# Two interleaved transformer layers on one core: V's weights arranged in finer pieces, early partial sums of layer 2 in one step, and new order tables

## The chip, the cores and the metric

The kernel runs on one core of one Trainium2 chip. The metric is device time in microseconds of one execution; lower is better. The core has five engines that run side by side, each in the order in which its instructions were written: TensorE (PE, matrix products; its weight loads are listed apart as PEld), VectorE (DVE), ScalarE (ACT), GpSimd (POOL) and SyncE (SP), which here only issues DMA transfers. They wait for one another through semaphores. A DMA transfer runs beside the engines once SP has issued it.

## The reference

The reference applies two layers to x, 2048 tokens of 512 values, each layer an attention block and a token-mixing MLP, with the same weights in both layers:

```python
x = A_x
x = x + _A_ref(_layernorm(x), A_wqkv, A_wo)
x = x + _B_ref(_layernorm(x), B_w1, B_b1, B_w2, B_b2)
x = x + _A_ref(_layernorm(x), A_wqkv, A_wo)
x = x + _B_ref(_layernorm(x), B_w1, B_b1, B_w2, B_b2)
```

`_A_ref` forms Q, K and V with one product (512 by 1536), splits them into 32 heads of 16, and lets each token attend to itself and the 255 tokens before it: scores times 16^-0.5, mask, softmax, weighted sum of V, and the output product with `wo` (512 by 512). `_B_ref` normalises again (the MLP's input is thus normalised twice), multiplies along the tokens, `u = gelu(w1^T h + b1)` with 1792 rows, and back to 2048 tokens, `y = w2^T u + b2`. All arrays are bf16.

## The kernel before

**How an order is written.** The kernel first records every operation in an object `Plan`: which engines could do it, what it reads and writes, and a priority. Nothing is run in the order of recording. A table `ORDER` (L27 on) holds, for each of the five engines, the list of its operations in the order in which they are to run, each operation's number packed into two characters. `arrange` decodes it, and `emit` writes every engine's instructions in that order and puts a semaphore wait before an operation for what it needs from others. So the order of the work, and which of two or three possible engines does an operation, is fixed by this table; the priorities in the code have no effect once the table is there. A second table, `BANKS`, says which of two spare PSUM banks (6 or 7) each use of a spare bank gets, and `misc_bank` (L476) hands them out.

**Attention.** The tokens are handled in four quarters of 512 (Q = 0 to 3), the heads in four tiles of eight heads (t = 0 to 3), and each pair of quarter and tile in nine steps (m = 0 to 8) over blocks of keys. For a step, `emit_scores` (L651) lets PE multiply K and Q into one of two score buffers of two PSUM banks each; `emit_exp` (L670) lets ACT exponentiate 128x1024 of them into `p_sb` (L672), after which DVE or POOL multiplies the edges of the window with 0 or 1 (L689); `emit_pv` (L697) multiplies with V, to which columns of ones are joined so that the sums of the softmax come out of the same product. After a tile's nine steps, the two result banks are copied to `oU` and `o2` (called `oU` and `o` in the profile) by `copy_out` (L332 on DVE, L334 on ACT). Every second tile, three small DMA transfers collect the sums into `den_c` and one of 256 KB moves rows of `o` into `oU`; the next copy into `o` waits for it. `job_inverse` (L734) and `job_normalise` (L744) divide, `job_outproj` (L625) multiplies with `wo` and adds to x. In between, `job_k`, `job_q` and `job_v` (L523, L529, L573) make K, Q and V of the next tile or quarter with `project` (L498), from the normalised tokens that were turned by DMA (`job_transpose`, L482) or, for the first quarter, by PE. The masked copies of K and Q stand at L514 (DVE) and L519 (ACT); V is copied to `vT`, turned 32 by 32 (L578) and spread into its tile (`spread_v`, L557; L563 DVE and POOL, L568 ACT).

**Weights of V.** The columns of V's weights have to stand in another order of heads than in memory. They are loaded as they are into a part of `w1buf`, and `turn_weights` (L407) copies them into `wqkv`, one operation for each chunk of 128 input values (c = 0 to 3), each of two instructions (r = 0, 1). `project` for V reads all four chunks and so waits for all four operations.

**MLP.** The 1792 rows are 14 tiles of 128 (`ft`). A tile's sum runs over all 2048 tokens, so over the four quarters. `u_product` (L826) makes four matmuls for each quarter. For six tiles (`NPART = 6`), the parts of the first two quarters are summed early, while the attention still runs on the later ones (`job_u_part`, L842): step 0 multiplies quarter 0 and copies the bank into room in `uT`; step 1 multiplies quarter 1 and adds bank and copy into `part`, which the profile calls `v_all` (L851). `job_u` (L864) later adds the rest (L872) and applies gelu (L875). For eight other tiles three quarters are summed ahead in PSUM. `job_y` (L878) makes the 16 token tiles of the result (matmul L900, addition to x at L904). Of layer 1's 16 tiles, the later ones run inside layer 2's attention. w1 comes in halves of 512 KB (`w1_half_dma`, L807) and pieces of 256 KB (`w1_dma`, L802), w2 in pieces of 896 KB (`w2_dma`, L822), into buffers that K, Q, the turned tokens and `oU` have left.

Of the kernel before, what the change touches and what calls it, by code (L numbers as in the profile page):

```python
# [8 lines left out]
ACTF = mybir.ActivationFunctionType  # L9

P = 128
# [4 lines left out]
NPART = 6  # L16
# [13 lines left out]
AoApAqArAsBHBJAtAuAvBLBNBPAwC-BTDiBRBVBnDRCcBzCaCmBrChAxC1CwCsBvC7DCClB3CvDIDMC0C6DVDBDHDLDcDTEDDkDqEcEwGODvDZD2FCF0DgDpDuEAD7DzEID1END6GgEYD-EHEMEhER  # L30
FXEnEsHJE1EgE6EmE-ErE0FHE5FMG5FTE+FGFLFaHjFQFvF2HWF7FZGAFuFzGGGKF6F-GRGFGJGQGUGbGqGjGiGnIAGtGmG0GsGzG3G7IOHAG-HEJbHMHDHLHTHQHYHcHgHpHsHbHfHwHoH4JzH9Hv
IGIyILH3H8IaJnIeIFIKImITKkIqIvHzI4IdIhIpIuI9I3I8JCJTJAKSJgJYIiJsK9JkJXJdJ4KuJwJjJrKJJvJ3J7J8LNKVKIKNLZKnKMKUKfKYLnKxKrM-KmK4MDK-KqKwLENGLIK3K7LQMQLWLD
LfLHLvLPLTLkLsNJLzLeLjL7LrLyLbMAL6L-MINQMNNeMbMfNoMHMnMMMUMrNuMvMeMiM3MqMuL2M8NCOlMjNLNVM2OMM7NbNBNlNIMyNrNSNzNOPkNaN3OENkNiNqOINyN2ORNYOcODOHOOOgOVQW
OnOrPLOyOfOkOqO4OxO1O-O3PDPaPIOPPQO+PXPTPCPHPNPdPhO8PrPWPcPwP2PmPgPqP+PvP1QFQmQPP9QTQ9QZQEQIQdP5QiQSQYQtRVQzQcQhQ3QqRBQsRIQyQ2Q8RMQCRSRFRaRPRfRLRRRkRZ
ReRjRyRxR1SpR2R3SyS1SzSqS2S4S5SBS0SsSEStSvSPSLS3STSHSrSwSjSxSuSkS-TLTBTFTMTDS6SlTPTbTTTcTUTfTQTgS7TXTYSmSnSoS9TJTHTuT+TzT0TvT5T6UnUoT-UiUMUjUVUTUNURUX
UbUZUgUcU0VKVAYVWbYWWcVTVOU4U8VhVcXwXxVIVSVmVtVZVEVyVbVgV2V7VlV+VsWFWgWwVxV1WSWNVqXPV9WjWCWXW+WoWtWJWRWWZeW-W6WiWnW1ZUWLXLXUWsW0XiXZW5XEXeYpX5XnXTXYXd
XsXmXrX2ZtYDX+aDYKX1YRZCYkX9YCYHYraEYwYOY1YQY6YjYoYvY0Y5Y9Y+ZFa0ZXZPZEa1abZIZbZhbeZoZvZWbfZ0ZaZgZnZ4cBaAZrZzaLa9aUZ3Z-aIaYbLahaTaXaoagaQawanava5a6aOZ9
bDbIcEbXbbdPbobCbHbQbscFbwbabjb5akb+brbvb4cRdhcWb9cecDcVcbcicxbkcqcubzcZc2chcpc6cldHctc1dLdsc5dSdGdcd7dkdKdRdpdVeLardvd2djeXd9dodud1eCekeGd5eOfBeUeBeF
edf+eheNepeRexeZe5ecegeoe+hMfGewe4fLe9fFesfZfKfSfdfOflgtfpftgde0f1fcfgfof7gNgBfsf0gKfhgUf6gAgagHgRgkhlingqgygFg2gZgjgphDfwhHgxg1hRiLhchChGhOhghVhngIhP
hrhyh8hfh4hkhqh-gPiDhxh3iIh1iQiXh+iTiCidiHiNihjWiriWiwicigiqi2ivi1iki+i9jEjFghjPjIjTiai5jZjdjmjijSjYjcjhjtgXjsjzj3gnjykIkVkBj2j8kFkSj9kMkfjCjqkakLkykR  # L40
kZkekjkkkPlykxk1k2k3lplzlsl1l4l2lvlEl5lwlBl0ltlHlLl6lTlPlxl3ljlklulllqmBmLmMmDlrmFmbmXmfl-mYmgmTmPmQmUmclmlnlol9l7mHmJmrm0m1mwmnmomxm9msnCm5m6nGnDnHm+
nPnTnLnMnQnUnXnbnfnnncngnjnYnqnk""",
    "vector": """
AaAbAUAcAYAdAZAzAeA1A0A2A7ASA+A5A3A6AfAWBEA9A4BBBABbBIBGBDBXBMBdBZBaAXAVBcAOBeBYAPAnATBfBhDjBSBWBjDSBpCbBsBqBtC3BuFgBwCkBxFeByCzB5DFB6FkFhFfFiFlEFEGEe
FjFmDKEfDaEyDfDPFDFoF1EzFqD0ECD+GhETEaESJDFYEbFEEqJFE8JEHKJGG6JHFVFRFSJJHkF5JIHXGDHlGWJKGVGrGTJNJLGdGlHmGpIBICGvGwGxIPG9G2G+JcHHHRHaHZHSHtHuIEHeHiJ0Hr
H6H7IQIzIRHyIIINISJ1IVJoI0IUKlIxI6H0JpJBKTIjI7JqJ2H1JPJeJfKvK+H2IkIlJ6J+KALOLaKZKCLoLpKpKEKhKtMEK0NAMFK6NHK1MRLSLYLwLVLhLULxNKLdLcNRMGL+NfNpMVMWMhMpNv
NwMSL3M6MTOmMxNxMtMkL4ONL5MzNTNgNPMlN1NnNhMmNjN6N7N9PlNZOWOKOBOAOTN-OLOiOCQXPMOuOvOtO2O6OwO7PBPFPbOQPKPVPGPUPPPOO9PZPfPSPtPoPnP4M0QnQHQoPzQRM1QKQJQ+RW
# [21 lines left out]
lilgmmmjmkmum3mqnBnAnJm4nSm8nFnWnenOnKmvnpnamznsninm""",  # L69
}  # L70
BANKS = (
    "76767676767667767776667767676767676666777667676766776777766676667666667767776766677777766766776677776676767776767776766666676666776767677677"
    "667666777767667676776677776677676777776676667677666667676767767666")


# [957 lines left out]
```

## Time and profile before

| what | us |
|---|---|
| median of 3 runs | 493.44 (492.94 to 494.23) |
| profiled execution, its own time | 493.72 |
| its span, first to last instruction | 492.0 |
| busy: PE / DVE / ACT / POOL | 467.4 / 339.1 / 322.5 / 192.1 |
| layer 1's attention ends, its MLP begins | about 163 |
| layer 2's attention begins to fill / ends | about 229 / 399 |
| TensorE clock granted | 1.0 throughout |

The span is shorter than the execution by 1.7 us, which lie around it. A group's line of the profile gives the line of the kernel, the engine, the operation, what it writes and reads, the count, the busy time in us and the mean duration of one in ns, and then the idle time just before these instructions with what ended it. A line of waits gives who waited for whom, the sum in us, how many times, and the longest. A line of windows gives the stretch and, for PE, PEld, DVE, ACT and POOL, the busy time and the instructions, then the granted clock, the share of the DMA engines and GB/s. The chain that ended last goes back from the end to what released each step.

### The profile page before, as it was taken

What the parts mean: (1) busy time and instruction counts of PE and PEld (TensorE: products, weight loads), DVE (VectorE), ACT (ScalarE), POOL (GpSimd) and SP (SyncE); (2) the same over time, 40 slices, a digit from 0 to 9 for tenths busy, and PEclk for the clock granted to TensorE, in tenths of its full rate; (3) what the DMA queues carried; (4) which work ended last, traced back from release to release, by engine and by line L of the source; (5) the groups of instructions that cost most, each with busy time, mean ns of one, the idle gap of its engine ahead of it and who ended that gap; (6) DMA issues with size and microseconds to landing.
All of it is one profiled execution on the core that took longest, in us unless ns stands there. A gap on an engine that the chain in (4) does not pass through costs nothing.

```text
span 492.0 us, 17498 instructions
## 1 busy us (share of the span) xinstructions
PE 467.4 (95%) x7610; PEld 255.9 (52%) x7706; DVE 339.1 (69%) x716; ACT 322.5 (66%) x394; POOL 192.1 (39%) x364
## 2 busy tenths in 40 slices
PE   8989889999999999999999999999999999999997
PEld 7444555555555444444445455555556554444444
DVE  7999999988897460246789868899878756121213
ACT  6889999999999303502688798999999940440000
POOL 5979775853314210002645513576354230000000
PEclk9999999999999999999999999999999999999999
DMA  6513319203013671505022500030300677050672
GB/s 214 87 66 79 81 5 113 69 6 112 27 46 92 181 223 50 151 0 151 2 44 79 141 27 3 29 53 19 112 15 16 182 211 217 23 151 0 174 201 96
DMA packets 82412, 43.61 MB, mean 89 GB/s; under 512 B 18720, under 2 KB 81312, under 8 KB 82336
## 3 DMA queue, kind: packets, MB, share of 16 engines
q1 hardware_dynamic: 78464, 42.48, 31.9%
q0 software_dynamic: 3872, 0.02, 1.5%
q8 instruction: 60, 0.98, 0.8%
q14 instruction: 16, 0.13, 0.1%
HBM read 32.51 MB, written 2.10 MB: 70 GB/s over the span
## 4 chain that ended last, share of the span: by engine, by line
PE 69%; DVE 14%; issue 5%; DMA 4%; ACT 4%; POOL 2%; SPq 1%; DVEq 0%; ACTq 0%; POOLq 0%
PE ps L832 19%; PE ps L900 18%; PE ps L503 10%; PE ps L661 9%; PE ps L710 8%; PE ps L630 4%; ACT p_sb L672 3%; DVE stats L439 2%; DMA oU<-o 2%; PE ps L754 1%; DVE q_sb L514 1%; DVE vT L332 1%; POOL p_sb L689 1%; DMA w1buf<-in_B_w_dram 1%; DVE vB L578 1%
## 5 line engine op out<-in xcount | busy, mean ns | idle before, releaser
L672 ACT ACTIVATE p_sb<-ps 128x1024 bf16<-128x1024 f32 (+8 forms) x288 | 261.0, 973 | 25.7 <-PE ps L661 20.4
L689 POOL TENSOR_TENSOR p_sb<-p_sb,edge 128x128 bf16<-128x128 bf16 (+2 forms) x233 | 107.4, 476 | 135.7 <-ACT p_sb L672 114.4
L661 PE MATMUL ps<-q_sb,k_sb 64*64 64x288 bf16 (+8 forms) x2816 | 106.6, 250 | 2.5 <-ACT p_sb L672 2.0
L503 PE MATMUL ps<-xhT,wqkv 128*128 128x512 bf16 x330 | 84.6, 380 | 7.0 <-issue 4.6
L710 PE MATMUL ps<-p_sb,v_all 64*64 64x288 bf16 (+8 forms) x2816 | 88.4, 246 | 2.6 <-DVE o L332 1.4
L661 PEld LDWEIGHTS ps<-q_sb,k_sb 64*64 64x64 bf16 x2816 | 52.9, 106 | 55.0 <-ACT p_sb L672 34.4
L710 PEld LDWEIGHTS ps<-p_sb,v_all 64*64 64x64 bf16 x2816 | 59.5, 107 | 15.2 <-issue 5.7
L900 PE MATMUL ps<-uT,w1buf 128*128 128x512 bf16 x272 | 62.4, 379 | 0.8 <-issue 0.5
L904 DVE SCALAR_TENSOR_TENSOR x_sb<-ps,b2col,x_sb 128x512 bf16<-128x512 f32 x31 | 22.6, 746 | 55.8 <-PE ps L900 55.7
L503 PEld LDWEIGHTS ps<-xhT,wqkv 128*128 128x128 bf16 x376 | 30.8, 97 | 39.3 <-issue 6.1
L689 DVE TENSOR_TENSOR p_sb<-p_sb,edge 128x256 bf16<-128x256 bf16 (+2 forms) x167 | 39.8, 257 | 9.6 <-ACT p_sb L672 7.8
L832 PE MATMUL ps<-xh_sb,w1buf 128*128 128x512 bf16 x175 | 43.3, 380 | 2.4 <-issue 1.5
L439 DVE BATCH_NORM_STATS2 stats<-x_sb 128x6 f32<-128x512 bf16 x64 | 43.0, 680 | 0.8 <-DMA x_sb<-in_A_x_dram 0.3
L900 PEld LDWEIGHTS ps<-uT,w1buf 128*128 128x128 bf16 x280 | 26.5, 98 | 32.2 <-issue 1.1
L514 DVE TENSOR_TENSOR q_sb<-ps,even 128x1024 bf16<-128x1024 f32 (+1 forms) x31 | 36.4, 1180 | 3.0 <-PE ps L503 2.5
L469 ACT ACTIVATE xh_sb<-x_sb,shift,rstd 128x512 bf16<-128x512 bf16 x9 | 7.2, 808 | 46.0 <-POOL shift L463 32.8
L459 POOL TENSOR_TENSOR rstd<-vare,mhalf 128x4 f32<-128x4 f32 x15 | 15.4, 1027 | 55.1 <-DVE nmean L461 48.3
L514 DVE TENSOR_TENSOR k_sb<-ps,half 128x1024 bf16<-128x1024 f32 x27 | 32.7, 1212 | 3.0 <-PE ps L503 2.1
L900 PE MATMUL ps<-uT,oU 128*128 128x512 bf16 x149 | 34.4, 379 | 0.3
L630 PE MATMUL ps<-wo_sb,oT 128*128 128x512 bf16 x113 | 29.4, 380 | 2.2 <-issue 1.3
L832 PE MATMUL ps<-xh_sb,k_sb 128*128 128x512 bf16 x124 | 30.2, 379 | 0.6 <-ACT p_sb L672 0.4
L832 PEld LDWEIGHTS ps<-xh_sb,w1buf 128*128 128x128 bf16 x192 | 16.9, 98 | 21.7 <-issue 1.9
(88 smaller groups left out, 461.9 us busy)
## 6 DMA issues: line engine op xcount, KB each, us to landing
w1buf<-in_B_w_dram SPq DMA_DIRECT2D x10, 896.0 KB
oU<-in_B_w_dram SPq DMA_DIRECT2D x6, 896.0 KB
w1buf<-in_B_w_dram SPq DMA_DIRECT2D x10, 512.0 KB
oU<-o SPq DMA_DIRECT2D x16, 256.0 KB
k_sb<-in_B_w_dram SPq DMA_DIRECT2D x16, 256.0 KB
q_sb<-in_B_w_dram SPq DMA_DIRECT2D x8, 256.0 KB
xhT<-in_B_w_dram SPq DMA_DIRECT2D x8, 256.0 KB
out_dram<-x_sb SPq DMA_DIRECT2D x15, 128.0 KB
```

The source lines that it names most:

```text
L439: dve(lambda e: e.bn_stats(stats[:, t, :], x_sb[:, t, :]), 690, prio, reads=[R("x", t)], writes=[R("stats", t)])
L459: pool(lambda e: e.tensor_tensor(rstd[:, sl], vare[:, sl], mhalf[:], op=ALU.pow), 1000, prio, reads=[R("vare", g), R("mhalf")], writes=[R( ...
L503: last = e.matmul(ps[:, b, :], lhsT=wqkv[:, c, c0:c0 + P], rhs=xhT[:, buf, c, :], start=(c == 0), stop=(c == 3))
L514: return e.tensor_tensor(dst, src.unsqueeze(2).to_broadcast([P, n, 2, w]), mask[:].unsqueeze(1).unsqueeze(3).to_broadcast([P, n, 2, w]), o ...
L630: last = e.matmul(ps[:, b, :], lhsT=oT[:, buf, t, i * P:(i + 1) * P], rhs=wo_sb[:, t, :], start=(t == 0), stop=(t == 3))
L661: last = e.matmul(ps[64 * c:64 * c + 64, 2 * half + r, 32 * i0:32 * i1], lhsT=k_sb[rows, ring, t, kb % 16, :], rhs=q_sb[rows, t, c, 32 * i ...
L672: latest[0] = plan.op({ACT: (170 + int(2 * (512 - c0) * 0.84), lambda e: e.activation(p_sb[:, slot, :, c0:512], ps[:, 2 * half:2 * half + ...
L689: return e.tensor_tensor(v, v, g, op=ALU.mult)
L710: last = e.matmul(ps[64 * r:64 * r + 64, B_O + (c ^ r), 32 * i0:32 * i1], lhsT=v_all[rows, col:col + 64], rhs=p_sb[rows, slot, r, 32 * i0: ...
L832: r = e.matmul(ps[:, b, :], lhsT=blk[:, n, (ft % 2) * P:(ft % 2 + 1) * P], rhs=xh_sb[:, 4 * g + n, :], start=(first and g == quarters[0] a ...
L900: r = e.matmul(ps[:, b, :], lhsT=blk[:, fc, (st % 2) * P:(st % 2 + 1) * P], rhs=uT[:, fc, :], start=(fc == 0), stop=(fc == NFT - 1))
L904: dve(lambda e: e.scalar_tensor_tensor(x_sb[:, st, :], ps[:, b, :], b2col[:, st:st + 1], x_sb[:, st, :], op0=ALU.add, op1=ALU.add), 750, prio,
```

## The change

Three things change.

- `turn_weights` is called for each head tile t and half r, eight operations of one instruction instead of four of two; a V projection reads the two of its own tile.
- In layer 2, the six early tiles have one step instead of two: the matmuls of quarters 0 and 1 go into the same bank, one after the other, and one copy takes the sum to `part`. In layer 1 the two steps stay. `NPART` becomes `NPARTS = (6, 6)`, one number for each layer.
- `ORDER` and `BANKS` are new throughout, for all five engines: other positions, and other engines for some operations. Only the first lines of SP's list are shown. Its first loads were, in order, x tiles 0, 1, 2 to 3, 4 to 7, then the weights of K, of V and of Q; they are now x tiles 1, 2 to 3, 0, then Q's weights, x tiles 4 to 7, K's and V's weights.

```diff
-NPART = 6
+NPARTS = (6, 6)
...
     "sync": """
-AAABACAGADAFAECqCgCuCrDhDQDoC5DGHIG4GeEUGfEXEVEWElGZGYGXGaDUK8KjIWIXHPLMIZIYKiKbKcKdKeKRMXMZMYItMaLiOYOZOaObPuP0QLQlQOQgQMPpQNRdQxRiR6R7R8R9OUGEOjRwTs
+ABACAAAEAGADAFCkCyDUCuDlCvC9DKG8GjEYGiEbHMDsEaEZDYGcGbGdGeKmEpIaIcKnIdIbGIHTLQLAKVKhKgKfKiMbMdMcMeOYOdOcOeOfIxPyQPQRQkQSQQPtP4QpRhR+Q-R-SASBRmSkOnR0Sl
...
-        def turn_weights(c):
-            d = wqkv[:, c, 2 * D:3 * D].rearrange("p (t a r d) -> p t r a d", t=4, a=4, r=2)
-            o = w_nat[:, c].rearrange("p (t r a d) -> p t r a d", t=4, r=2, a=4)
-
-            def f(copy):
-                def g(e):
-                    for r in range(2):
-                        last = copy(e)(d[:, :, r], o[:, :, r])
-                    return last
-                return g
-            plan.op({DVE: (500, f(lambda e: e.tensor_copy)), POOL: (1000, f(lambda e: e.tensor_copy)),
-                     ACT: (900, f(lambda e: lambda a, b: e.activation(a, b, ACTF.Copy)))},
-                    reads=[R("w1", 2, 0)], writes=[R("wqkv", 2, c)], prio=-96)
-        for c in range(4):
-            turn_weights(c)
+        def turn_weights(t, r):
+            d = wqkv[:, :, 2 * D + t * P:2 * D + (t + 1) * P].rearrange("p c (a r d) -> p c r a d", a=4, r=2)[:, :, r]
+            o = w_nat[:, :, t * P + 64 * r:t * P + 64 * r + 64].rearrange("p c (a d) -> p c a d", a=4)
+            plan.op({DVE: (250, lambda e: e.tensor_copy(d, o)), POOL: (400, lambda e: e.tensor_copy(d, o)),
+                     ACT: (360, lambda e: e.activation(d, o, ACTF.Copy))},
+                    reads=[R("w1", 2, 0)], writes=[R("wqkv", 2, t, r)], prio=-96)
+        for t in range(4):
+            for r in range(2):
+                turn_weights(t, r)
...
-            pe(f, 866, prio, reads=([R("wqkv", 2, c) for c in range(4)] if which == 2 else [R("wqkv", which)]) + [R("xhT", buf, i) for i in range(4)],
+            pe(f, 866, prio, reads=([R("wqkv", 2, (c0 - 2 * D) // P, r) for r in range(2)] if which == 2 else [R("wqkv", which)]) + [R("xhT", buf, i) for i in range(4)],
...
-        def job_u_part(ft, step, prio):
+        def job_u_part(ft, step, prio, whole=False):
...
-            u_product(ft, b, (PARTQ[step],), prio, late=[R("xh", sc) for sc in range(4 * PARTQ[step], 4 * PARTQ[step] + 4)])
-            if step == 0:
+            quarters = PARTQ if whole else (PARTQ[step],)
+            u_product(ft, b, quarters, prio, late=[R("xh", sc) for q in quarters for sc in range(4 * q, 4 * q + 4)])
+            if whole:
+                copy_out(part, ps[:, b, :], b, prio, 680, [R("part", ft)] + held)
+            elif step == 0:
                 copy_out(early, ps[:, b, :], b, prio, 680, kept)
...
-            for ft in range(NPART):
-                todo.append((base + 55 + 0.5 * ft, lambda p, ft=ft: job_u_part(ft, 0, p)))
-                todo.append((base + 60 + UP0 + UPD * ft, lambda p, ft=ft: job_u_part(ft, 1, p)))
+            for ft in range(NPARTS[L]):
+                if L == 0:
+                    todo.append((base + 55 + 0.5 * ft, lambda p, ft=ft: job_u_part(ft, 0, p)))
+                todo.append((base + 60 + UP0 + (20 / NPARTS[L] - 0.03) * ft, lambda p, ft=ft, L=L: job_u_part(ft, 1, p, L == 1)))
```

By the decoded tables the instructions of PE (7708) and SP (178) stay as many; DVE has 727 for 718, ACT 395 for 396, POOL 351 for 368. The lines of the changed kernel behind L425 are smaller by about five.

## The prediction

> **What bounds the kernel now.** First the page's busy line, then the windows by stage, then the waits, the groups with shapes kept apart, and the chain of work that ended last. [...] Of the page's first part:
>
> ```profile
> PE 467.4 (95%) x7610; PEld 255.9 (52%) x7706; DVE 339.1 (69%) x716; ACT 322.5 (66%) x394; POOL 192.1 (39%) x364
> ```
>
> The windows (PE, PEld, DVE, ACT, POOL busy in each stretch) show the stages:
>
> ```profile
> 10.00:20.00 10.00, 9.65 (x100) 5.44 (x99) 9.85 (x25) 8.55 (x16) 9.25 (x22) 1.00 0.18 44
> 20.00:40.00 20.00, 17.81 (x298) 9.02 (x295) 19.59 (x41) 17.87 (x28) 17.32 (x39) 1.00 0.43 87
> 40.00:60.00 20.00, 17.56 (x415) 10.13 (x418) 18.72 (x42) 18.08 (x23) 17.18 (x38) 1.00 0.31 81
> 60.00:80.00 20.00, 18.35 (x516) 11.45 (x512) 18.15 (x38) 19.57 (x23) 12.52 (x19) 1.00 0.31 44
> ...
> 163.00:205.00 42.00, 41.68 (x252) 18.99 (x253) 15.68 (x30) 12.15 (x19) 3.85 (x6) 1.00 0.57 161
> ...
> 320.00:350.00 30.00, 28.41 (x748) 17.36 (x758) 28.05 (x55) 29.02 (x33) 19.66 (x35) 1.00 0.21 41
> 350.00:380.00 30.00, 28.48 (x768) 17.38 (x766) 24.64 (x51) 28.31 (x32) 16.26 (x30) 1.00 0.17 47
> 380.00:399.00 19.00, 18.21 (x385) 10.50 (x388) 14.13 (x35) 16.10 (x20) 6.32 (x12) 1.00 0.73 200
> 399.00:440.00 41.00, 40.63 (x244) 18.78 (x248) 15.61 (x31) 11.73 (x19) 2.77 (x5) 1.00 0.50 139
> ```
>
> From 10 to 60 us DVE leads (98%, 98%, 94%); from 60 to 163 us, the rest of layer 1's attention, ACT does, with its exponentials (19.57 of 20 in the first of these windows); both MLPs (163 to 229, 399 to 492) are PE alone; layer 2's attention is shared by PE and ACT, ACT ahead from 320 us on. The waits (us in total, times, longest) say the same:
>
> ```profile
> PEld ps L661 <- ACT p_sb L672: 34.4, 84, 0.8
> ACT p_sb L672 <- PE ps L661: 20.4, 39, 3.2
> ...
> PE ps L710 <- DVE o L332: 1.4, 2, 1.2
> DVE o L332 <- DMA oU<-o: 1.4, 2, 1.2
> ```
>
> PE stands 84 times before a score matmul because both score buffers are still with the exponential; ACT stands 39 times because PE is late. Two waits of 1.2 us hang on the reload of half of oU by DMA; they and one late w1 load are in the chain (start, us):
>
> ```profile
> 45.15 4.44 DMA oU<-o
> ...
> 80.27 4.13 DMA oU<-o
> ...
> 349.18 6.54 DMA w1buf<-in_B_w_dram
> ```
>
> The prices, from the groups with shapes apart:
>
> ```profile
> L332 DVE COPY uT<-ps 128x512 f32<-128x512 f32 x11 | 7.6, 687 | 3.0 <-PE ps L832 2.8
> L851 DVE TENSOR_TENSOR v_all<-uT,ps 128x512 f32<-128x512 f32 x12 | 8.1, 676 | 0.0
> L418 ACT ACTIVATE wqkv<-w1buf 128x256 bf16<-128x256 bf16 x4 | 1.3, 404 | 0.0
> L414 POOL COPY wqkv<-w1buf 128x256 bf16<-128x256 bf16 x2 | 0.7, 390 | 0.0
> ```
>
> **The change part by part.** The sum is made against the profiled execution: 493.72 us, of which the span is 492.0 and 1.7 lies around it; it stands 0.28 above the median 493.44.
>
> *V's weights.* Eight copies of the same size before and after. Before 4 on ACT, 2 on POOL, 2 on DVE (350 ns), after 3, 3 and 2: ACT -0.4, POOL +0.4, DVE 0. What is new is the tie: a V projection needs its own tile's two copies, not all eight. No row shows a V projection waiting for them. Taken at 0; bounds -0.4 (ACT's piece) to +0.4 (POOL's piece).
>
> *Layer 2's early partial sums.* Before, each of six feature tiles has a copy (five at 687 on DVE, one on ACT at 612) and an add (676 on DVE): DVE 5 x 0.687 + 6 x 0.676 = 7.5 us. After, one copy each, four on DVE and two on ACT: 2.7 us. DVE -4.8, ACT +0.6. The copies lie between 355 and 399 us, where DVE is busy 24.64 of 30 and 14.13 of 19: mostly beside other work. PE's matmuls stay (48 x 0.216 = 10.4 us), but quarter 0's now wait to stand beside quarter 1's. By the two written orders, PE has 2.2 us less ahead of the end of the third quarter's attention and in the fourth quarter 34.1 us of work where it had 31.0, in a stretch of 36.1 us; ACT gets 1.5 more there. The bank of a sum is held over 2.2 to 4.5 us of PE work instead of 0.9, with at most one other user of the two spare banks in between (a K projection, an output projection), so the second bank covers it. The third quarter's end (320 to 363) is full on DVE, ACT and PE alike, so the 2.2 us are worth something between 0 and 2.2: I take 1.3. The fourth quarter's extra 3.1 fits in its slack of 36.1 - 31.0 = 5.1, and costs 0 to 3.1: I take 0.6, as ACT there still idles 4.6 of 49.
>
> *The tables: starting up.* x4:8 is loaded behind q and k is behind both. Landings of the first loads in the trace: slot by slot 2.85, 3.53, 4.67, 6.31, 9.21, 10.66, 12.00. x4:8 moves from the fourth slot to the fifth, +2.9 us; the statistics of x4 to x7 move with it, DVE's queue behind them holds the masks of K and Q and so the first exponential (16.36). Walked through by rows, ACT's chain of its K and Q parts still sets that exponential, at about 16.2 to 16.3; DVE is then 1.5 to 2 us behind, with 2.0 us less to do before the second quarter begins. In return SP issues the second quarter's transposes earlier: the last landed at 26.24 and its projection ran at 27.32; by SP's order it lands near 23.4 (an estimate: the same 1.2 us of issue each, started where the first x load no longer goes between). I take -1.2 for the stretch to 60 us, where DVE is the bound and has 1.5 us less in layer 1; bounds +2.0 (the backlog is never made good) and -2.8 (the whole earlier landing).
>
> *The tables: layer 1's attention.* By rows, ACT gets +1.9: five oU copies (600 each) and a partial sum (612) come, three o copies (603) go, a K mask (two of about 0.69) comes, V spreading (-1.05) and the turn (-0.4) go. POOL has 2.3 less. ACT is the bound from 60 us on, but the windows from 20 to 163 us leave it 9.3 us of idle. At 0.5 of its price: +0.9; bounds 0 to +1.9. The oU reloads: the first has 5.1 us of PE work from trigger to user, where it had 6.3, but goes ahead of one transpose (1.2 us of issue) that it stood behind; the second has 8.0 for 8.8, with a transpose still ahead. Two waits of 1.2 us stay as they are: 0; bounds -2.4 to +1.2. Layer 1's first w1 half is issued some 22 us later and keeps 28 us of lead: 0; if that cover went, it would cost its 3.5 us flight.
>
> *The tables: layer 2's loads.* The w1 half that was 6.54 us in the chain gets 21.7 us of lead for 6.9: its wait of 0.6 goes. Late next is the second w1 block's first half: on SP it stands behind the other half and a small load of the sums' denominators that waits for the o and oU copies of the third quarter, so it cannot go before these; from there PE has 6.04 us of work until it needs the half. Wanted: about 2 for the copies and queue, 1 of issue, 3.8 of flight (rows of 3.5 to 4.1 alone), 6.8 in all: a wait of +0.8, between 0 and 3.3 (two halves at once took 6.0 to 6.5). If it waits, PE's queue behind it holds the next score matmuls and ACT runs dry. The w2 block before the last output tiles has 6.05 for about 5.5 (4.85 alone), covered; with two at once (7.0) it would cost 1.0. V's spreading leaves ACT (-5.4 between the layers, mostly where ACT idles anyway), POOL has 6.8 less, DVE 3.0 less inside the attention: worth -1.0 where 320 to 350 is full on all; bounds 0 to -3.0.
>
> [...]
>
> Layer 2: -1.3 + 0.6 - 0.6 + 0.8 - 1.0 = -1.5. The end is unchanged: same last output tile, same store. Sum: -1.2 + 0.9 - 1.5 = -1.8, 493.72 - 1.8 = 491.9, and by the median **491.6 us**, own range 488.5 to 491.9.
>
> **The rivals.**
>
> *A wash (493.0).* The layers' attention keeps its pace: copies hidden, ACT's +1.9 absorbed, and what PE no longer does early it does late. For it: total work falls by only 1.6 us on DVE and 0.5 on ACT, PE's not at all. Against: DVE is at 94 to 98% for 50 us. Within 0.3%, which is about what a measurement of this kernel can tell from no change.
>
> *ACT decides (slower, 495.4).* Layer 1's +1.9 is paid in full, and the fourth quarter's +1.5 takes 0.6 of what the third gave: 493.44 + 1.9 + 1.5 x 0.4 - 0.5 = 495.4. It decides if ACT is above 97% from 60 to 163 us. For it: 19.57 of 20 in one window, 21.97 of 23 in another; against: 17.97 of 20 at 100 to 120.
>
> *The late w1 half (slower, 495.6).* Its wait is 3.3, as with two transfers at once, and there is no gain elsewhere but 1.1: 493.44 + 3.3 - 1.1. It decides from a landing later than 7.1 us after the third quarter's last score buffers are out, since PE is in order.
>
> *POOL's relief reaches DVE (faster, 489.5).* The edge masks on DVE run 142 to 710 ns: masks of 217 ns alone have taken 710 beside a POOL instruction. By shape the masks average 304, 240 and 205 where 283, 215 and 182 are usual, the spreads 755 and 520 for 683 and 417: over their counts (72, 43, 52, 16, 7) an excess of 5.7 us. POOL does about 9 us less of 192.1, 5%: 0.3 us by proportion; if every microsecond of POOL's stood in DVE's way, the 2.3 less of layer 1 would come off DVE's bound stretch: 491.6 - 2.1 = 489.5.
>
> ```profile
> L689 DVE TENSOR_TENSOR p_sb<-p_sb,edge x167: 142/238/710, 21.6 to 397.1; 128x256 bf16<-128x256 bf16 x72, 128x64 bf16<-128x64 bf16 x52, 128x128 bf16<-128x128 bf16 x43
> ```
>
> [...]
>
> **How the numbers follow.** Forecast 0.40, POOL's relief 0.05, wash 0.17, ACT 0.22, late half (with the starting backlog) 0.16. Faster by over 0.3% 0.45, within 0.3% 0.17, slower 0.38. The range: below, to the bounds of the start and layer 2 in part, 488.8; above, beyond both slower cases by 0.6, 496.2.
>
> **What would show it.** Right: the second quarter's first projection before 26.5 us; L851 six times instead of twelve and six copies fewer in all; no w1 load of over 6 us in the chain near 349; the windows from 20 to 60 with DVE below 96%. Wrong: the first exponential after 17.5 us; a wait of PE for w1buf above 1.5 us near 365; ACT over 98% from 60 to 163 with a later end of layer 1's attention than 163; PE in 363 to 399 no fuller than before.

## The result and the profile after

The changed kernel is slower: 498.47 us at the median (495.9 to 500.13, 9 runs) beside 493.44 (492.82 to 496.74, 9 runs) for the kernel before on the same chip, a ratio of 1.0089, 95% interval 1.006 to 1.0118. That lies outside the stated range of 488.8 to 496.2. Its profiled execution took 497.17 us, 3.45 more than the one of before (493.72).

The busy line of its page:

```profile
PE 467.6 (94%) x7606; PEld 255.5 (52%) x7706; DVE 340.6 (69%) x725; ACT 322.8 (65%) x393; POOL 184.1 (37%) x347
```

PE and ACT have as much to do as before within 0.3 us, DVE 1.5 us more; POOL has 8 us less. So most of the loss is waiting; what VectorE's 1.5 us are is told further down. The windows by stage (PE, PEld, DVE, ACT, POOL busy, then clock, DMA share, GB/s) show where:

```profile
20.00:40.00 20.00, 17.76 (x297) 9.24 (x300) 19.69 (x39) 17.80 (x28) 19.58 (x42) 1.00 0.35 66
40.00:60.00 20.00, 17.19 (x373) 9.53 (x376) 18.36 (x38) 17.31 (x23) 12.67 (x32) 1.00 0.36 67
...
80.00:100.00 20.00, 16.90 (x413) 9.90 (x419) 17.80 (x35) 17.01 (x19) 13.59 (x20) 1.00 1.62 127
100.00:120.00 20.00, 19.17 (x508) 11.87 (x510) 18.29 (x37) 18.99 (x22) 6.08 (x11) 1.00 0.05 18
120.00:163.00 43.00, 41.00 (x1079) 25.00 (x1088) 36.66 (x86) 41.79 (x46) 17.17 (x30) 1.00 0.23 68
...
350.00:380.00 30.00, 27.66 (x706) 16.78 (x708) 24.65 (x52) 28.32 (x31) 16.70 (x26) 1.00 0.31 90
380.00:399.00 19.00, 18.21 (x455) 10.98 (x453) 12.21 (x30) 17.38 (x21) 5.72 (x11) 1.00 0.42 126
```

From 80 to 100 us all three attention engines fall together, while the DMA share goes up to 1.62 from 0.59. The same window of before:

```profile
80.00:100.00 20.00, 19.10 (x451) 10.93 (x456) 19.21 (x36) 19.19 (x22) 15.67 (x27) 1.00 0.59 82
```

When all three stand at once, the wait is likely to be for something outside them. The waits between 82 and 95 us name it:

```profile
ACT p_sb L667 <- PE ps L656: 2.8, 2, 2.2
...
PE ps L498 <- DMA xhT<-xh_sb: 1.9, 1, 1.9
```

PE stands 1.9 us before a V projection (L498) of the fourth quarter, because the normalised tokens turned by DMA (xhT) are not there; ACT stands behind it, and so does DVE, whose copy of that projection waits 2.1 us for PE. The chain of work that ended last (start, us) has the same place:

```profile
84.03 1.25 SPq L479
...
85.33 6.04 DMA xhT<-xh_sb
...
91.63 0.59 PE ps L498 x2
```

What the forecast watched has come otherwise. The two 1.2-us waits for the oU reload are gone from the list of waits, and two others stand where they stood:

```profile
PE ps L498 <- DMA xhT<-xh_sb: 3.0, 2, 1.9
...
DVE o L333 <- DMA den_c<-o: 1.6, 1, 1.6
```

The second is at 48 us, the wait for the sums' transfer. In layer 2 the w1 half of 6.54 us is out of the chain; by the trace the two halves there land 3.7 and 4.7 us after their issue ends. The late half of the second block lands at 369.73, and PE takes it up at 369.77:

```profile
PEld ps L827 <- DMA w1buf<-in_B_w_dram: 0.3, 1, 0.3
```

To place the loss I took from both traces the end of each attention tile (its last PV product) and formed the delay against before, less what the two orders differ by in PE work done up to there. In us, of after and of the runs told below (a plus is late; Q0t1 is layer 1's first quarter, tile 1, "L2" layer 2; "MLP 1" is the start of layer 1's first output tile, 204.85 us before the change; "end" is the end of the span):

```
             Q0t1   Q0t3   Q1t2   Q1t3   MLP 1  L2 Q2t0 L2 Q2t1 L2 Q3t1  end
after        +0.14  +1.06  +0.67  +2.77  +2.67   +2.31   +2.35   +3.22  +3.45
e1           +1.70  +2.66  +2.25  +2.42  +2.95   +2.70   +3.36   +4.62  +4.94
e2           -0.06  +0.06  -0.34  +1.00  +0.69   +0.74   +2.02   +2.97  +3.19
e3           +0.05  +3.08  +2.70  +2.80  +3.52   +3.13   +3.79   +4.82  +5.16
e4           +0.40  +2.16  +1.74  +3.50  +3.13   +2.93   +3.59   +4.48  +4.66
e5           +1.41  +1.41  +0.97  +4.83  +5.09   +4.84   +4.88   +5.79  +6.10
e6           +1.61  +1.27  +0.83  +1.00  +1.70   +1.31   +2.00   +3.13  +3.33
h1           +0.42  +0.74  +0.30  +0.48  +0.98   +0.60   +1.88   +2.69  +2.91
h2           +0.22  -0.27  -0.71  -0.60  +0.02   -0.36   -0.33   +0.71  +0.93
g1           +0.08  -1.09  -1.08  -1.35  -1.38   -1.39   -0.68   -0.84  -0.85
```

In after, the first tile ends 1.4 us earlier than before by this measure, and the next has already lost it; 0.9 goes by 56 us, of which 0.4 is made good by 83 us; 2.1 goes between 83 and 94 us, and 1.1 in layer 2 from Q2t0 on. These are single executions, and a row scatters by up to a microsecond or two at the start, as will be seen; the steps within a row say more than its end.

### The profile page after: what moved, and what is told of

Same layout as the page of the kernel before. It is cut to its first block, busy times and chain, and to the rows that moved or that the text cites. A ratio compares the mean times of both kernels' runs of the same rounds, so it can differ in the third digit from the quotient of the medians.

```text
span 495.4 us, 17479 instructions
## 1 busy us (share of the span) xinstructions
PE 467.6 (94%) x7606; PEld 255.5 (52%) x7706; DVE 340.6 (69%) x725; ACT 322.8 (65%) x393; POOL 184.1 (37%) x347
## 4 chain that ended last, share of the span: by engine, by line
PE 68%; DVE 13%; DMA 6%; issue 4%; SPq 3%; ACT 3%; POOL 1%; DVEq 0%; ACTq 0%
PE ps L900 18%; PE ps L827 14%; PE ps L498 11%; PE ps L656 10%; PE ps L705 8%; PE ps L625 4%; ACT p_sb L667 3%; SPq L327 3%; DMA den_c<-o 2%; DVE k_sb L509 2%; DMA xhT<-in_B_w_dram 2%; DVE p_sb L684 2%; DVE o L333 1%; DMA x_sb<-in_A_x_dram 1%; DMA xhT<-xh_sb 1%
## 5 line engine op out<-in xcount | busy, mean ns | idle before, releaser
L667 ACT ACTIVATE p_sb<-ps 128x1024 bf16<-128x1024 f32 (+7 forms) x288 | 262.6, 972 | 29.3 <-PE ps L656 26.3
L684 POOL TENSOR_TENSOR p_sb<-p_sb,edge 128x256 bf16<-128x256 bf16 (+2 forms) x218 | 104.2, 492 | 123.8 <-ACT p_sb L667 95.0
L498 PE MATMUL ps<-xhT,wqkv 128*128 128x512 bf16 x326 | 85.3, 380 | 12.0 <-issue 3.8
L684 DVE TENSOR_TENSOR p_sb<-p_sb,edge 128x256 bf16<-128x256 bf16 (+2 forms) x182 | 48.9, 285 | 11.8 <-ACT p_sb L667 11.4
L498 PEld LDWEIGHTS ps<-xhT,wqkv 128*128 128x128 bf16 x376 | 30.6, 97 | 43.3 <-issue 6.0
L827 PE MATMUL ps<-xh_sb,w1buf 128*128 128x512 bf16 x177 | 44.4, 380 | 2.0 <-issue 1.6
L509 DVE TENSOR_TENSOR q_sb<-ps,even 128x1024 bf16<-128x1024 f32 (+1 forms) x29 | 34.4, 1193 | 4.0 <-PE ps L498 3.7
L509 DVE TENSOR_TENSOR k_sb<-ps,half 128x1024 bf16<-128x1024 f32 (+1 forms) x27 | 32.1, 1191 | 2.5 <-PE ps L498 1.7
L872 DVE TENSOR_TENSOR v_all<-v_all,ps 128x512 f32<-128x512 f32 x12 | 8.2, 687 | 32.1 <-PE ps L827 32.1
```

Source lines behind the costliest of these rows:

```text
L498: last = e.matmul(ps[:, b, :], lhsT=wqkv[:, c, c0:c0 + P], rhs=xhT[:, buf, c, :], start=(c == 0), stop=(c == 3))
L509: return e.tensor_tensor(dst, src.unsqueeze(2).to_broadcast([P, n, 2, w]), mask[:].unsqueeze(1).unsqueeze(3).to_broadcast([P, n, 2, w]), o ...
L667: latest[0] = plan.op({ACT: (170 + int(2 * (512 - c0) * 0.84), lambda e: e.activation(p_sb[:, slot, :, c0:512], ps[:, 2 * half:2 * half + ...
L684: return e.tensor_tensor(v, v, g, op=ALU.mult)
L827: r = e.matmul(ps[:, b, :], lhsT=blk[:, n, (ft % 2) * P:(ft % 2 + 1) * P], rhs=xh_sb[:, 4 * g + n, :], start=(first and g == quarters[0] a ...
```

## The experiments

All edits are lines in `arrange`, put in behind the decoding of the table: `s`, `a`, `v`, `g` are SP's, ACT's, DVE's and POOL's lists by place. Line numbers in their profiles are larger by the lines put in. Each ratio is to the kernel before, run beside that run on the same chip (its medians there were 493.45 to 494.62 us). My theory after the result: layer 1's fourth quarter waits for its last two DMA transposes because the new table puts two w1 halves ahead of them on SP. The rivals: a small load of the biases (b1col, issued by POOL at 83.95 us) slows them; or all of it is layer 2, and what layer 1 loses would be made good.

**Transposes ahead of the halves (e1).**

```diff
+        s[36:40] = s[38:40] + s[36:38]
```

> The changed kernel with one edit in SP's list: the last two transposes of layer 1's fourth quarter are issued before the two w1 halves that stood ahead of them. Theory A (these halves, 512 KB each, hold the transposes up, which took 5.56 and 4.50 us to land and let PE and ACT stand for 2 us each at 90 to 92 us): the transposes land within 3.5 us of their issue, the end of the second quarter's attention comes about 2 us earlier (93.6 to 91.5), and the time falls by about 2 us, to some 495.2. Theory B (the small load of b1col, issued by POOL at 84.0 in the same moment, 7 KB in many small packets, holds them up): the transposes still take over 4 us and the time stays at 497.

Measured: 496.87 (495.57 to 498.67, 6 runs), ratio 1.0065 [1.0043, 1.0087]. The step between Q1t2 and Q1t3 falls from +2.1 to +0.2 us. The two transposes land 3.18 and 2.01 us after their issue ends, where they took 5.56 and 4.50, and the windows no longer have the hole (e1, in 5-us windows; first after, then e1):

```profile
85.00:90.00 5.00, 4.46 (x111) 2.44 (x111) 5.00 (x9) 4.96 (x6) 3.34 (x6) 1.00 5.07 184
90.00:95.00 5.00, 3.16 (x66) 1.86 (x72) 2.80 (x9) 2.78 (x4) 3.17 (x6) 1.00 0.53 116
```

```profile
85.00:90.00 5.00, 4.69 (x102) 2.52 (x108) 5.00 (x8) 4.46 (x6) 4.20 (x5) 1.00 1.76 57
90.00:95.00 5.00, 4.65 (x126) 2.75 (x128) 4.79 (x12) 4.69 (x6) 3.83 (x7) 1.00 0.99 263
```

**The bias load later (e2).**

```diff
+        g.insert(156, g.pop(130))
```

> The changed kernel with one edit in POOL's list: the load of b1col is issued some 40 us later, where no transposes are on the way. Theory B (this load's small packets hold up the transposes): they land within 3.5 us, the second quarter ends about 2 us earlier and the time falls by about 2 us, to 495.2; the DMA share of 5.07 between 85 and 90 us goes. Theory A (the w1 halves do): transposes still over 4 us, time unchanged at 497.

Measured: 496.56 (495.42 to 497.14, 6 runs), 1.0054 [1.0035, 1.0073]. The same step is +1.3 instead of +2.1, and the transposes land 4.52 and 3.69 us after their issue: the 7 KB load, which took 7.2 us to land in after and 4.4 in before, has a part of about 0.8 in the step; the halves have more.

**Both (e3).** The two edits together.

> Both edits at once: transposes ahead of the w1 halves and b1col 40 us later. By theory A or B alone it is as fast as the one of the two single edits that helps, about 495; if each holds up a part, it is faster than either by about 1 us. What remains above the kernel before (493.4), about 1.5 us, would then be for the start and layer 2 to explain.

Measured: 497.3 (495.95 to 498.89, 6 runs), 1.0072 [1.0049, 1.0094]. The step is +0.1 us and the two transposes land in 1.11 and 1.20 us, as before's did when alone: here the theory holds, both parts of it: with the halves and the bias load the transposes took 5.56 and 4.50 us, with the halves alone 4.52 and 3.69, with the bias load ahead 3.18 and 2.01, without either 1.11 and 1.20. But the time is no better than with either edit alone, and none of the three intervals lies clear of that of the changed kernel: what is shown here is shown by the traces. The profiled execution, the longest of the six, lost 3.0 us elsewhere, between Q0t1 and Q0t3 (after: 0.9), where the third quarter's last transpose was late as well (windows of e3, 2 us each):

```profile
48.00:50.00 2.00, 0.32 (x2) 0.32 (x4) 0.30 (x1) 1.32 (x2) 1.37 (x4) 1.00 0.58 143
50.00:52.00 2.00, 1.48 (x28) 0.90 (x29) 1.56 (x3) 0.70 (x1) 0.42 (x1) 0.87 0.39 126
52.00:54.00 2.00, 2.00 (x44) 1.62 (x37) 2.00 (x7) 1.25 (x2) 0.69 (x2) 0.50 0.00 0
54.00:56.00 2.00, 1.67 (x38) 0.98 (x36) 1.07 (x5) 1.14 (x2) 0.56 (x2) 0.77 0.04 8
```

PE has 0.32 of 2 us at 48, and after that the granted clock (third figure from the right) stands at 0.87, 0.50 and 0.77. So there is a second place of the same kind, and a price that I had not counted: the clock.

**x tiles 4 to 7 ahead of Q's weights (e4); the third quarter's transposes ahead of reload and wo (e5); e5 and e1 together (e6).**

```diff
+        s.insert(3, s.pop(4))
```
```diff
+        s[19:29] = [s[20], s[19], s[22], s[23]] + s[25:29] + [s[21], s[24]]
```

> The changed kernel with the load of x tiles 4 to 7 issued ahead of Q's weights, as before the change. Theory C (the late x4 to x7 leave VectorE a backlog that the first quarter never makes good): x lands about 2 us earlier, the first quarter's second tile (38.85 us) ends 1 to 1.5 us earlier, the time falls by 1 to 1.5 us, to 496. Rival: VectorE is busy without a gap from 10 to 45 us either way, so the order of its work changes and not its sum, and Q's weights now hold the first exponential back (15.2 to about 16.3 us): time unchanged within 0.5 us.

> The changed kernel with one edit in SP's list in the first quarter: the last transpose of the second span (the third quarter's tokens) is issued before the oU reload instead of behind it, and the two loads of wo go behind the next tile's four small transfers. Theory D (copies in flight beside a transpose make both slow, and VectorE's o copy and PE's V projection wait 1 to 2 us each at 48 to 51 us): the transpose lands by 47 us, the stretch from the first quarter's third to its fourth tile gets 0.6 to 2.7 us shorter (it took 9.5, 9.5, 8.7, 11.6 and 10.3 us in five profiles), the time falls by about 1 us, and its scatter between executions with it. Rival: the reload now lands as late behind the transpose as in the kernel before (3.8 us) and the o copy waits 1.2 us as there: no gain beyond 0.3 us.

> The edit of the first quarter and the one of the transposes ahead of the w1 halves at once. If the two collisions on the DMA queue are what layer 1 loses, the MLP's first output tile comes within 0.7 us of the kernel before (204.85 us; 2.67 late in the changed one), and the time is 493.5 + what layer 2 loses (0.8 to 2.5 in five profiles), 494.3 to 496. If ACT's 1.9 us more work in layer 1 is the loss, the first output tile stays 2 us late and the time at 496 or more.

Measured: e4 498.29 (496.9 to 500.79), 1.0101 [1.0073, 1.0129]; e5 497.93 (497.16 to 499.83), 1.0073 [1.0057, 1.0088]; e6 497.04 (495.7 to 497.29), 1.0053 [1.0038, 1.0069], 6 runs each. e5 ends the loss at 46 to 56 us (from Q0t1 to Q0t3 0.0, after +0.9, e3 +3.0), but alone it gains little, as the second quarter's last tile then loses 3.9 us: PE stands 2.6 us from 90.05 on for the fourth quarter's transposes, and the clock goes (windows of e5):

```profile
90.00:92.00 2.00, 0.05 (x4) 0.00 (x0) 0.85 (x2) 1.13 (x2) 1.90 (x4) 1.00 1.39 67
92.00:94.00 2.00, 1.32 (x17) 0.70 (x22) 0.31 (x1) 0.00 (x0) 0.60 (x1) 0.91 0.71 206
94.00:96.00 2.00, 1.95 (x48) 1.48 (x42) 0.89 (x5) 1.75 (x2) 0.97 (x2) 0.50 0.22 65
96.00:98.00 2.00, 1.72 (x28) 0.76 (x29) 2.00 (x5) 0.68 (x2) 0.00 (x0) 0.74 0.00 0
```

With both places mended (e6), layer 1 has no large step left after Q0t1. Yet e6 misses what was expected of it: the first output tile is 1.7 us late where 0.7 was allowed, and the time is not below 496. The rival there was ACT's extra work along layer 1; but of the 1.7 us, 1.6 are there at Q0t1 already. What e6 shows is the start: its Q0t1 is +1.6 late, and so are e1's and e5's, which do not touch the start. In all three x tiles 4 to 7 landed later than after's 8.88 us (10.12, 9.56 and 9.98 in e1, e5 and e6), and PE stood 1.46 us for them. e4 removes that: in h1 and h2, which contain it, they landed at about 7.5 to 8 and were taken up at 8.7, without a stand. Alone, e4 shows no gain: its profiled execution stands at +0.4 at Q0t1, where after's quick one stood as well, and then loses 1.8 us by Q0t3 and 1.8 at 83 us.

**Four more copies (e7).** In e6's kernel, DVE copies the bank of four of layer 2's one-step sums once more, to a place that nobody reads: 4 x 0.69 = 2.7 us of DVE work, about what the change takes from it there.

> As the run with both edits in SP's list, and in layer 2 four more copies of an early sum on VectorE (4 x 0.69 = 2.7 us), each right before the copy that the one-step form has; their output is not used. If evictions of the early sums lie on the path, it is 1.5 to 2.7 us slower than that run; if they are hidden beside PE and ACT, within 0.5 us of it, and the one-step form is worth nothing by them.

Measured: 497.27 (496.41 to 498.48, 6 runs), 1.0065 [1.0048, 1.0081], beside e6's 1.0053: intervals overlap. In the traces the stretch from layer 2's Q2t2 to the end costs 0.8 us more. So, by these two executions, the copies that the change takes away were worth about 0.8 of their 2.7 us at most; the rest was beside other work.

**All mended places (h1, h2).** h1 is e1, e4 and e5 together; h2 also has the bias load later and, in layer 2, the oU reload ahead of two small transfers:

```diff
+        s.insert(111, s.pop(113))
```

> The changed kernel with both edits of layer 1's list on SP, and x tiles 4 to 7 loaded ahead of Q's weights as before the change. Theory E: in the changed kernel VectorE has nothing left to do when x tiles 4 to 7 come, so the scatter of their landing (8.8 to 10.1 us in eight profiles) goes straight into the start, 1.5 us between the quick profiles and those where PE stands 1.46 us at 9.9 us. With x first there is no such stand, the first quarter's second tile ends within 0.5 us of the kernel before beyond its other work, and the time is 0.5 to 1 us below the run with the two edits alone (ratio 1.0053 to the kernel before): 1.003 to 1.004. Rival: the single edit of the x load showed no gain beside the others (ratio 1.0101 for 1.0089), so the first exponential now waits for Q's weights: 1.005 as without it.

> As the run before, and two more edits: b1col's load 40 us later on POOL, and in layer 2 the small transfer that the second quarter's oU reload waits for is issued first of three, so that the reload is issued about 1 us earlier. Theory D (transfers collide and VectorE and PE wait for them) says that the wait at 336 us (1.1 us in two of five profiles) goes too: ratio 1.002 to 1.003. Rival: the transfer must wait for its copies on ACT and blocks the other two: no gain.

Measured, 12 runs each: h1 495.59 (494.35 to 496.79), 1.0029 [1.0017, 1.0041]; h2 495.36 (494.4 to 496.72), 1.0027 [1.0017, 1.0038]. By the order of SP and POOL alone the excess of 0.0089 goes down to 0.0027, clear of the changed kernel's interval; h2 came as expected, h1 just below it. In the trace h2 stands at -0.3 up to L2 Q2t1; its reload there is issued at 330.35 and lands at 332.88, and the step of about +1.3 that h1 and e2 have at Q2t1 (their DVE waits for it) is gone. What is left comes in layer 2's fourth quarter.

**V's finer tie taken back (h3).** h1 with V projections that wait for all eight pieces, and the late pieces moved forward on their queues:

```diff
-[R("wqkv", 2, (c0 - 2 * D) // P, r) for r in range(2)]
+[R("wqkv", 2, t, r) for t in range(4) for r in range(2)]
+        a.insert(11, a.pop(14)); a.insert(12, a.pop(16))
+        v.insert(39, v.pop(46)); g.insert(18, g.pop(20))
```

> As the run with the start too, but each V projection waits for all eight pieces of V's weights, as before the change, and the eight pieces therefore stand together on their engines, ahead of the first exponentials. Theory: the finer tie lets ACT put two pieces of 0.4 us between its first exponentials, behind which they cost the same 0.8 us; nothing waits for V's first projection: within 0.5 us of the run with the start too. Rival: the first exponentials come 0.8 us later and all that follows with them: 0.8 us slower.

Measured: 496.52 (495.55 to 497.0, 6 runs), 1.0045 [1.0031, 1.0059], 0.9 us above h1, and in the trace 1.0 us later at Q0t1: the first exponential comes at 16.37 us instead of 15.47, behind three pieces on ACT. So the rival was right, and this part of the change, done as it is, gains about 0.9 us at the start, though the two intervals still overlap. (The pieces moved forward are part of that price; the two were not separated.)

**The same moves in the kernel before (g1, g2).** g1 puts before's oU reloads earlier and its w1 half and bias load later; g2 also swaps two transfers in layer 2.

```diff
+        s[24:29] = s[25:29] + [s[24]]
+        s[34:39] = [s[36], s[37], s[35], s[38], s[34]]
+        g.insert(160, g.pop(127))
```
```diff
+        s[119:121] = [s[120], s[119]]
```

> The kernel before with its own collisions taken out: in the second quarter the oU reload is issued ahead of a transpose, and the w1 half behind the transposes; in the first quarter the w1 half goes behind the next tile's small transfers; b2col is loaded some 15 us later. Theory D says that the two waits of 1.2 us of VectorE for the reload (at 49.6 and 84.4 us) go: 1 to 2 us faster, 491.5 to 492.5. Rival: the waits are hidden, since VectorE and ACT catch up later: within 0.3%.

> The kernel before with the four edits of its first trial (ratio 0.9984, interval 0.9965 to 1.0003) and in layer 2 the two w1 halves swapped, so that the one that PE needs first (its 6.54 us stand in the chain, its wait was 0.6 us) is issued first. Theory D: 1.2 to 2 us faster than the kernel before, ratio 0.9965 to 0.9975. Rival: the waits that go are filled by others: 0.999.

Measured, 12 runs each: g1 493.61 (492.88 to 494.82), 0.9984 [0.9965, 1.0003]; g2 493.95 (492.33 to 494.6), 0.9993 [0.9981, 1.0006]. In g1's trace both 1.2-us waits for the reload are gone and layer 1 ends 1.4 us earlier, but that execution is the fastest of the twelve, and the times cannot be told from before's: theory D missed, its rival was right. No kernel of this study is faster than before beyond its interval.

**The one-step sums alone (k1, k2, k3).** What was left in h2 lies where layer 2's early sums lie. So the one-step form went into the kernel before, alone. In k1 quarter 0's matmuls stand just ahead of quarter 1's, at the places of the latter; k2 brings five of the pairs, with their copies, forward to about the places of the changed kernel; k3 is k1 with one or more other PE steps between any two blocks of four matmuls. Table, loads and engines are before's.

```diff
+        for ft, o0, o1, c in self.pair:            # k1: o0 is quarter 0's block, o1 quarter 1's
+            t.remove(o0)
+            t.insert(t.index(o1), o0)
...
+        behind = {1: (753, 615), 2: (766, 622), 4: (791, 637), 3: (807, 645), 5: (816, 651)}   # k2: places on PE, DVE
...
+        ahead = {0: t[747], 1: t[755], 2: t[789], 3: t[816], 4: t[818], 5: t[827]}             # k3
```

> The kernel before with one part of the change alone: in layer 2 the six early sums in one step, quarter 0's matmuls just ahead of quarter 1's, at the place where quarter 1's stand; everything else as before. It takes away six copies (five of 687 ns on DVE, one of 612 on ACT) and moves six times 0.864 us of PE work 1 to 34 places later. The theory that the form itself costs what is left in the mended kernels (+0.8 in the fourth quarter): from the end of the third quarter's tile 2 to the end of the kernel +0.8 against before, ratio 1.0016 to 1.003. The theory that the copies were worth something, as the forecast had it (-1.3 + 0.6): -0.7, ratio 0.9986. The rival that it is all hidden: within 0.3 us, ratio 0.9994 to 1.0006.

> As the run before it, but with both quarters' matmuls and the copy where the changed kernel has them: five of the six pairs earlier, between the two places that the kernel before gives to the two steps. PE's work is then spread as in the changed kernel. If the fuller fourth quarter of the run before it costs (theory one), this one loses less: +0.3 to +0.5, ratio about 1.001; if the form is hidden, both are the same within 0.3 us; if the copies were worth something, -0.7 here too.

> As the run with the one-step form at the late places, but the two quarters' matmuls of a sum no longer stand side by side: every block of four (0.864 us) has a score or PV step between it and the next, as in the changed kernel, so the work of PE is the same and nearly at the same places. The theory that the loss of 3.6 us comes from 1.7 to 3.5 us of such matmuls in a row, over which ACT runs out of scores: from the third quarter's end +0.5 to +1.5 against before, ratio 1.001 to 1.003. The theory that it comes from the work that PE no longer does early, or from the one copy's place: as in that run, +3 to +4, ratio 1.006 to 1.008.

Measured, 6 runs each: k1 498.19 (496.86 to 498.79), 1.0072 [1.0049, 1.0094]; k2 503.44 (502.92 to 508.33), 1.0209 [1.0174, 1.0245]; k3 498.6 (497.87 to 500.47), 1.0093 [1.0062, 1.0124]. None of the three numbers expected of k1 comes near. That k1's blocks stand side by side is not the cause, since k3 loses as much; of k3's two theories the second was nearer, that the work which PE no longer does early costs, or the place of the one copy. k2 is another case: it holds the spare banks too long, and output projections wait for the copy (k2, 362 to 404 us):

```profile
PE ps L652 <- DVE v_all L354: 2.1, 2, 1.8
```

It shows nothing on the form but that a badly placed copy costs more than the form does.

For k3, the same stretch first of before, then of k3:

```profile
ACT p_sb L672 <- PE ps L661: 2.3, 4, 0.9
...
PEld ps L661 <- ACT p_sb L672: 2.3, 6, 0.4
```

```profile
ACT p_sb L690 <- PE ps L679: 6.1, 10, 1.0
...
PEld ps L679 <- ACT p_sb L690: 6.6, 14, 0.9
```

Both waits have grown by about 4 us: PE stands longer for the exponentials, and ACT longer for the scores. The ends of tiles tell the order. k3 is 0.7 us late at the end of Q3t2 and 4.4 at the end of Q3t3 (k1: 2.0 and 4.6). Up to the first of these marks before had already made three blocks (3 x 0.864 = 2.6 us) that k1 and k3 make behind it. From there to Q3t3 k1 loses 2.6 us, just these three blocks, and k3 3.8. So quarter 0's blocks had stood in before where PE waits for ACT anyway, and cost little there; moved behind, they stand where PE is late, and cost in full, and the early places stay empty. The place of the copy is a small part of it: in 362 to 404 us the trace shows one wait of 0.4 us for it in k1 and in k3. In all k1 loses 3.8 us and k3 4.6, counted from the end of Q2t2, where they stood at +0.8 and -0.1; what goes beyond the three blocks, 1.2 and 2.0 us, is not accounted for. The changed kernel's tables place these blocks otherwise (its two waits in that stretch are 2.6 and 3.6 us) and lose less; h2's PE is busy 19.00 of the 19 us from 380 on, where before's was 18.21, and it still ends later.

## Why the prediction was wrong

The forecast was 491.6 us, with 0.45 for faster; the profiled execution lost 3.45 us where the sum had -1.8. By the table of delays the stretch up to 83 us came out at +0.7 (forecast -1.2), the step between 83 and 94 us at +2.1 (no term), the rest of layer 1 at -0.1 (+0.9), and from layer 1's first output tile to the end at +0.8 (-1.5). The range was too narrow by its own terms: its upper end of 496.2 was taken from the two slower rivals, while the upper bounds of the start and of layer 1 alone (+2.0, +1.9, +1.2) come to +5.1; likewise the forecast's own range ended 0.3 us above the forecast.

*Layer 1's first w1 half, "keeps 28 us of lead: 0".* This is the step whose failure the runs show best, and it cost 2.1 us. The lead was right (the half lands at 77.94, its user starts at 99.68). The sum costs the moved loads by their own users and not by what they meet: with the first half, two others moved too, to 82.25 and 82.73 us, right ahead of two transposes on the same queue, and in flight together with them and b1col's load. These have no term in the sum. Landing times for that were in the trace of before: most transposes there landed 1.1 to 1.3 us after their issue, the one at 77.94 us, beside a w1 half and b2col's load, after 3.42. None of the rivals has this. e1, e2 and e3 show it.

*"I take -1.2 for the stretch to 60 us".* It was +1.1 at 56 us and +0.7 at 83. The first exponential came at 15.16 instead of 16.36, as hoped and more; the second quarter's first projection at 26.74 instead of 27.32, not before 26.5. But the first tile's 1.4 us were lost by the second tile, and every profile of the new tables loses about 1.5 us there, from whatever start: DVE is busy 9.81 of 10 and 19.69 of 20 us, so an earlier ACT only waits. The forecast's own reading, DVE bounds from 10 to 60 us, would have said so. What failed in it is "has 1.5 us less in layer 1": the window from 20 to 40 did not fall below 96%, and less work on DVE shows only in 40 to 60 (18.36 for 18.72). That sum goes by before's rows, and their mean durations did not hold. For the masks, before and then after:

```profile
L689 DVE TENSOR_TENSOR p_sb<-p_sb,edge 128x256 bf16<-128x256 bf16 x72 | 21.0, 304 | 4.4 <-ACT p_sb L672 4.3
L689 DVE TENSOR_TENSOR p_sb<-p_sb,edge 128x128 bf16<-128x128 bf16 x43 | 10.2, 240 | 2.8 <-ACT p_sb L672 1.5 <-POOL p_sb L689 1.3
```

```profile
L684 DVE TENSOR_TENSOR p_sb<-p_sb,edge 128x256 bf16<-128x256 bf16 x66 | 22.2, 341 | 5.8 <-ACT p_sb L667 5.7
L684 DVE TENSOR_TENSOR p_sb<-p_sb,edge 128x128 bf16<-128x128 bf16 x59 | 15.9, 280 | 2.1 <-ACT p_sb L667 1.9
```

The excess of DVE's masks and spreads over the usual durations (283, 215, 182, 683, 417 ns, as in the last rival) was 5.6 us in before and is 12.0 in after; from 20 to 60 us it goes from 1.0 to 3.1. All eleven profiles of the new tables have 11.8 to 13.3, those of before and its variants 5.1 to 6.4, and every mask or spread that is over 50 ns too long runs beside a POOL instruction (27 in before and 47 in after; 56 and 53 others run beside one and are not). In size this is what the start lacks; no run takes it away, so that it is the cause there is not shown. In addition there came, at 46 us, the third quarter's last transpose, put behind the oU reload: 2.83 us to land where it took 1.22, at 48.83 instead of 46.27.

*The oU reloads, "two waits of 1.2 us stay as they are: 0".* Both went, and the waits for transposes and den_c took their place. What the two were worth is not shown: g1, without them, gains 1.4 us by the end of layer 1 in one execution and nothing that its times can show.

*V's finer tie, "taken at 0", bounds ±0.4.* About -0.9 by h3, a gain outside the bounds, with the reserve that its interval overlaps h1's. What was missing is that the tie lets ACT do pieces behind its first exponentials: in after at 17.0 and 18.1 us, where before had all four done by 12.0.

*ACT's +0.9.* Not paid: from 94 us on the delay no longer grows in layer 1 (+2.77, and +2.67 at the first output tile), and ACT is busy only 0.3 us more over the whole. (The pieces that the forecast lists add up to 1.7, not 1.9.) The rival that ACT decides falls with it; ACT is at 97.2% from 120 to 163 us, but at 95% from 100 to 120.

*Layer 2, -1.5.* It was +0.8 in after from the first output tile on, +1.1 from L2 Q2t0 on, and +1.3 in h2, from Q2t1 on. The 6.54-us load went, as said. The late w1 half made PE wait 0.3 us, not 0.8 (and not the 3.3 of the rival); the flight was 3.97 us, as the rows had it, and it was issued earlier than I had reckoned. That the evictions lie mostly beside other work held (e7). What failed is "the fourth quarter's extra 3.1 fits in its slack", for which I took 0.6, and with it the relief of 1.3 ahead of it: k1 and k3 show that this slack is not free, as PE's idle time there is waiting for ACT, at other moments than those at which the work comes; in k1 a block of 0.86 us put behind cost about 0.86. The forecast's last sign of being wrong came true as well: from 363 to 399 us PE is busy 33.83 us, where it was 34.43, and not fuller. Whether all that is left in h2, 1.3 us, comes from the form is not shown, since its tables differ from before's in other ways there as well.

*POOL's relief.* The reverse came: POOL has 8 us less (184.1 for 192.1), and yet DVE's masks run longer beside it, by the rows above. So in these two traces the excess (12.0 for 5.6 us) does not go by how much POOL does. DVE's total, forecast 1.6 us lower, rose by 1.5; the 6.4 us of added excess are more than this difference. (In that rival's price 2.1 is subtracted where 2.3 is named.)

That the times scatter over 4 us was not in the sum either: the four longest of the nine executions, 498.9 to 500.1 us, have a mean clock of 0.997, the others 1.0.

## What to carry to other kernels

A moved load is costed twice: by its lead to its own user, and by every short transfer that now stands behind it or flies beside it and has a user close by; here the two transposes were 2.1 us. Work that fills an engine's waiting time can cost its full duration as soon as it is moved out of there, however idle the new place looks in a window's mean: k1's three blocks of 0.864 us cost 2.6. An earlier start of one engine, 1.4 us at the first tile, was worth nothing here up to the next engine that is busy without a gap. And a mean duration taken from the old order need not hold in the new one: masks of the same shape took 9 to 17% longer, by shape, in the mean.

## What the runs showed of the hardware

- The DMA transposes of 128 KB took 1.2 to 2.4 us to issue in before and after. With nothing else in flight, 117 of 124 of them over all traces landed 1.1 to 1.3 us after that, the others 2.1 to 3.0 us (in before and after alone 17 of 19, the others 2.1 and 2.5). Beside loads, the oU reload or other transposes they landed after 1.1 to 4.1 us; beside two w1 halves after 4.5 and 3.7 (e2), and beside these and the bias load after 4.4 to 5.8 (after, e4, e5).
- The granted clock fell to half for 3.41 us at a time: in e3 from 51.49 us on, in e5 from 93.63 us on. It falls again behind the end of PE's work, at 498.64 and 499.81, which is 131 and 119 times 3.413 us later. The records at full clock of before and after, from 5.46 and 5.64 us to the falls at 493.57 and 497.16 behind the end, are 488.106 and 491.519 us long, 143 and 144 times the same 3.413. In the 3.41 us ahead of the two early falls PE was busy 1.29 us (e3, behind a stand of 1.7 us) and 0.95 (e5, a stand of 2.6). After's stand of 1.9 us is longer than e3's, and its clock stayed at 1.0. Counted back from its last fall in steps of 3.413, a border would lie at 90.97 (an estimate, 119 steps), in the middle of that stand, and PE was busy 2.03 and 2.55 us in the two steps beside it. In before and after the step ahead of the last fall held no work of PE, and each other one from 5.46 and 5.64 us on held 2.03 us or more. Counted in the same way, the most work ahead of a half clock was 1.38 us (k2, at its end), and the least that none followed 1.93 (e4, at 46.74). What decides between the two was not shown.
- A fall of 3.41 us costs PE at most 1.7 us of work (an estimate, half of 3.41). e3's stand of 1.7 us brought one, after's of 1.9 us did not.
- The landing of the same x tiles, fifth in the same queue at the same issue time (2.71 us), was 8.77 to 8.88 us in three executions and 9.56 to 10.12 in four others, and passes through to the end of the second tile (Q0t1 is at -0.06 to +0.14 in the three, and at +1.4 to +1.7 in e1, e5 and e6, three of the four).
- DVE's masks of 128x256, of two inputs each, took 227 to 293 ns in after where no POOL instruction ran beside them (36 of 66), and up to 1104 ns beside one (at 76.65 us).
